# First pair of heads loaded on two queues and projected first, activation table behind the loads

## Chip, cores and metric

One core of a Trainium2 chip runs the kernel. The metric is the device time of one execution in microseconds (us), the median of several.

## What is computed

Linear attention over 8 batches and 8 heads of 576 tokens (64 wide) and then a mixture of experts on the 4608 rows that come out. Cut to what matters here:

```python
def phi(x):                                   # x: q or k, (8, 8, 576, 64)
    proj = einsum('bhsd,df->bhsf', x, w_phi)  # w_phi: 64 x 128
    proj = proj - max(abs(proj), axis=-1)
    return concat([exp(proj), exp(-proj)])
q_p, k_p = phi(q), phi(k)
kv  = einsum('bhsf,bhsd->bhfd', k_p, v)
z   = sum(k_p, axis=2)
num = einsum('bhsf,bhfd->bhsd', q_p, kv)
den = einsum('bhsf,bhf->bhs', q_p, z) + 1e-6
x   = num / den, as rows of 512               # 4608 x 512
# then: rows with x @ w_skip > 0 go through the expert of the largest gate
# logit (512 -> 1024 -> 512, relu), all others pass unchanged
```

## The kernel before

The attention goes through 16 units of four heads (`units["k"]`, `units["q"]`); a unit is two pairs of heads, numbered pr 0 and 1. The last tokens of each head (2 of every 18) are kept apart: they make a third, small piece of each unit, the tails, whose tiles end in t (`xTt`, `ut`, `ekt`).

- **Loads.** `st_load` (L330) brings a unit of k or q into `raw`. The first units come in eight DMAs of 72 KB, four for each pair (two heads by two halves of 32 columns), at L347; from unit 2 on k comes in four DMAs of 280 KB (L343). `st_loadv` brings v in five DMAs (L355 four times, L361). All are issued by SyncE (its queue is SPq), but for the first units: the second pair of the first k unit (argument `more`) and the whole first q unit are issued by ScalarE (ACTq), which also loads `w_phi` into `wsrc` (L824) ahead of them.
- **DMA semaphores.** The DMAs of both queues use eight semaphores in turn, DMAHW0 to DMAHW7, in the order in which the scheduler places them. A DMA that gets a semaphore a second time is issued only when the DMA that had it before has landed.
- **Projection.** VectorE transposes `raw` into `xT` (pair) and `xTt` (tails of the unit) at L384. `st_proj` multiplies them by `wsrc` on TensorE (L395) into one of two PSUM buffers `ps_A`, and VectorE takes the largest magnitude (`m`, L405) and subtracts it (`u`, L406), which frees `ps_A`. The third projection in a row therefore waits until `u` (or `ut`) of the first is done.
- **Use.** ScalarE makes `ekt` and `ek` from `ut` and `u` (L420). TensorE sums them with v into `ps_K` (`st_use_k`, L476). For q, `u` is transposed and used against the sums (L428, L545).
- **Order.** The main loop runs steps t = 0, 1, 2, ...; each step handles one pair of k and one of q (two steps later), and the letters of `CFG["order"]`, alternating by the parity of t, say in what order its pieces are emitted: `0` is the projection of the tails, `1` that of a k pair, `2` that of a q pair, `a`, `b`, `c`, `d` VectorE's work for them. `CFG["ends"]` replaces the string for single steps. Steps 0 to 2 are still ordered by the scheduler; from step 3 on the order written here stands.
- **Activation table.** A one-element `Exp` on the tile `warm` (L105), ahead of everything on ScalarE, brings the table in early.

The functions that the change touches:

Of the kernel before, what the change touches and what calls it, by code (L numbers as in the profile page):

```python
# [13 lines left out]
AF = mybir.ActivationFunctionType  # L14
# [4 lines left out]

P = 128  # L20
SLOT = 256
CFG = {'late': 1, 'sp': 1, 'gp': (6, 8, 11, 14, 16, 19, 21), 'rows': 9.0, 'tab': (2, 2, 3, 4, 5, 6, 7, 8, 9, 10, 11, 12, 15, 19, 31), 'ql': 0, 'cp': 0, 'seq': ('E', 'E', 'E', 'C', 'C', 'SC', 'C', 'DS', 'C', 'D'), 'post': (4, 8, 6), 'post2': (3, 5, 5), 'pk': (0, 2, 4), 'man': (3, 38), 'eng': ('PE', 'DVE', 'Activation', 'Pool'), 'nb': {'K': 1, 'O': 1, 'A': 2, 'P': 3, 'U': 2}, 'apools': (('ld', 2), ('hl', 4), ('up', 5), ('zp', 2), ('ep', 7), ('kvp', 5), ('ac', 1), ('xp', 3)), 'mpools': (('wseta', 1), ('mx', 1), ('mo', 2), ('wsetb', 1), ('wsetc', 1), ('rawq', 1)), 'lag': (2, 2, 3, 0), 'order': ('LPv12KQebRcdBuExzwlr', 'LP01aKQ2ebRcdBuExwzyr'), 'vl': 0, 'at': 1, 'eb': (2, 2), 'ub': 4, 'stage': (2, 2, 4, 4), 'stage2': (1, 2, 3, 3), 'dve': ('0', '1', 'ntkq', '2', 'n2', 'tkq', 'n2t'), 'pd': 1, 'vq': 0, 'qq': 1, 'xb': 4, 'whole': 'k', 'vb': 1, 'af': 1, 'wg': 2, 'q0': 1, 'out6': 2, 'ends': {34: '2dcvQeuEFBwlLRPr', 35: 'QcueERwyLXPr', 36: 'cuwRyLPr'}}


@with_exitstack
def kernel(
# [256 lines left out]
    with actx:  # L285
        ld, hl, zp, up, ep, kvp, xp = (pools[nm] for nm in ("ld", "hl", "zp", "up", "ep", "kvp", "xp"))
# [17 lines left out]
        units = {"k": [], "q": []}  # L304
        for b in range(B):
            for hq in range(NQ):
                for kind in ("k", "q"):
                    u = Unit()
# [18 lines left out]
                c.pop(0)()  # L327
                last = c

        def st_load(u, eng=nc.sync, more=None):  # L330
            whole = u.kind in CFG["whole"]
            w = D if whole else 32
            whole = whole and u.g >= CFG["wg"]
            u.raw = ld.tile([P, 2, 18, w], F32, tag="raw" + u.kind, name="raw", bufs=2)
            for pr in range(1 if whole else 2):
                for hd in range(2):
                    for dh in range(2):
                        r = slice((2 * hd + dh) * 32, (2 * hd + dh) * 32 + 32)
                        src = kv_in[u.kind][u.g][hd * 32:hd * 32 + 32]
                        if whole:  # L340

                            n = 18 * D - 32
                            nc.sync.dma_start(  # L343
                                out=u.raw[r].rearrange("p r t c -> p r (t c)")[:, :, 0:n],
                                in_=src[:, :, dh * 32:dh * 32 + n])
                        else:
                            (more if more and pr == 1 else eng).dma_start(  # L347
                                out=u.raw[r, pr, :, 0:32],
                                in_=src[:, pr].rearrange("p (t c) -> p t c", c=D)[:, :, dh * 32:dh * 32 + 32])

# [483 lines left out]
        man = None
        pend = []
        for t in range(NPR + F + LQ + 2):
            if t == CFG["man"][0]:
                man = ExitStack()
# [33 lines left out]
            qx, mx, kb = [], {}, []  # L872
# [386 lines left out]
    for grp in CFG["seq"]:  # L1259
# [17 lines left out]
    order = sorted(begin, key=begin.get)  # L1277
# [48 lines left out]
    two = [x for x in order if x[0] != "S"]  # L1326
# [125 lines left out]
```

## Time and profile before

| | us |
|---|---|
| median of 3 runs | 581.87 (579.68 to 582.03) |
| the profiled execution, its own time | 578.38 |
| its span, first to last instruction | 576.2 |
| TensorE busy | 522.2 (91%) |
| VectorE busy | 447.4 (78%) |
| ScalarE busy | 341.9 (59%) |
| GpSimd busy | 282.7 (49%) |

The span leaves out 2.2 us around the first and last instruction. Busy shares are means over the whole kernel, the attention and the experts together; the change lies within its first steps, so the rows that matter are those of the first 40 us.

### The profile page before, as it was taken

What the parts mean: (1) busy time and instruction counts of PE and PEld (TensorE: products, weight loads), DVE (VectorE), ACT (ScalarE), POOL (GpSimd) and SP (SyncE); (2) the same over time, 40 slices, a digit from 0 to 9 for tenths busy, and PEclk for the clock granted to TensorE, in tenths of its full rate; (3) what the DMA queues carried; (4) which work ended last, traced back from release to release, by engine and by line L of the source; (5) the groups of instructions that cost most, each with busy time, mean ns of one, the idle gap of its engine ahead of it and who ended that gap; (6) DMA issues with size and microseconds to landing.
All of it is one profiled execution on the core that took longest, in us unless ns stands there. A gap on an engine that the chain in (4) does not pass through costs nothing. (4 is left out here: it accounts for less than half of the span.)

```text
span 576.2 us, 20682 instructions
## 1 busy us (share of the span) xinstructions
PE 522.2 (91%) x8606; PEld 485.4 (84%) x8606; DVE 447.4 (78%) x790; ACT 341.9 (59%) x606; POOL 282.7 (49%) x520
## 2 busy tenths in 40 slices
PE   2888999998999898998989999799999989999993
PEld 2788999888998888998988898699889878988892
DVE  3887788988778887797966897778879898868840
ACT  1457676677666776677665443745676757646620
POOL 4213335635547354564546256683749571558011
PEclk9989999999999999999999999899999999999998
DMA  7878878788987989875367895679577986867400
GB/s 147 176 166 163 168 160 211 194 170 174 243 205 194 195 174 224 201 183 122 130 211 270 251 335 179 180 247 335 167 254 241 325 289 233 276 205 250 171 20 32
DMA packets 151233, 116.25 MB, mean 202 GB/s; under 512 B 91875, under 2 KB 126819, under 8 KB 150114
## 3 DMA queue, kind: packets, MB, share of 16 engines
q1 hardware_dynamic: 140704, 104.51, 66.7%
q0 software_dynamic: 3200, 9.45, 4.6%
q10 hardware_dynamic: 7234, 0.95, 1.0%
q8 instruction: 69, 1.13, 0.8%
q14 instruction: 26, 0.21, 0.1%
HBM read 91.66 MB, written 24.02 MB: 201 GB/s over the span
## 5 line engine op out<-in xcount | busy, mean ns | idle before, releaser
L217 POOL TENSOR_TENSOR w<-wraw_c,w 128x256 fp32r<-128x256 f32 x84 | 81.1, 994 | 54.2 <-ACT w L212 38.4
L405 DVE TENSOR_REDUCE m<-ps_A 128x8 f32<-128x1024 f32 x64 | 77.0, 1203 | 35.7 <-PE ps_A L395 35.7
L217 DVE TENSOR_TENSOR w<-wraw_c,w 128x1024 fp32r<-128x1024 f32 x71 | 94.0, 1340 | 12.8 <-ACT w L212 12.5
L212 ACT ACTIVATE w<-wraw_c 128x1024 fp32r<-128x1024 f32 x92 | 93.8, 1050 | 7.4 <-DMA wraw_c<-in_moe_w_dram 7.4
L476 PE MATMUL ps_K<-vm,ek 128*64 128x65 f32 x2048 | 79.9, 224 | 5.4 <-issue 3.0
L406 DVE TENSOR_TENSOR u<-ps_A,m 128x1024 f32<-128x1024 f32 x64 | 78.3, 1224 | 3.9
L545 PE MATMUL ps_O<-kva,eq 128*64 128x74 f32 x1984 | 76.8, 229 | 4.6 <-issue 4.0
L395 PE MATMUL ps_A<-wsrc,xT 64*128 64x128 f32 x1024 | 73.1, 289 | 7.2 <-DVE u L406 4.5
L476 PEld LDWEIGHTS ps_K<-vm,ek 128*64 128x64 f32 x2048 | 73.0, 140 | 5.5 <-issue 4.7
L545 PEld LDWEIGHTS ps_O<-kva,eq 128*64 128x64 f32 x1984 | 68.8, 136 | 8.2 <-issue 4.6
L395 PEld LDWEIGHTS ps_A<-wsrc,xT 64*128 64x128 f32 x1024 | 65.8, 199 | 10.2 <-DVE u L406 4.8
L437 ACT ACTIVATE eq<-ps_V 128x1024 f32<-128x1024 f32 x64 | 65.7, 1030 | 9.6 <-PE ps_V L428 9.6
L420 ACT ACTIVATE ek<-u 128x1024 f32<-128x1024 f32 x64 | 64.1, 1057 | 2.3 <-DVE u L406 2.3
L1110 PE MATMUL ps_O<-w,hh 128*128 128x512 f32 x160 | 63.7, 398 | 0.0
L1029 POOL DMA_INDIRECT out_dram<-o,si x22 | 28.8, 1307 | 59.5 <-DVE si L1025 46.0
L549 ACT ACTIVATE os<-ps_O 128x296 f32<-128x296 f32 x62 | 26.1, 420 | 48.4 <-PE ps_O L545 46.4
L1115 PE MATMUL ps_O<-w,hlo 128*128 128x512 f32 x120 | 47.2, 394 | 0.0
L1114 PE MATMUL ps_O<-w,hh 128*128 128x512 f32 x120 | 47.0, 391 | 0.0
L524 POOL TENSOR_TENSOR xm<-os,rec 128x512 f32<-128x512 f32 x32 | 33.4, 1045 | 24.9 <-DVE rec L523 21.5
L384 DVE STREAM_TRANSPOSE xT<-raw 128x512 f32<-128x512 f32 x64 | 40.5, 669 | 1.2 <-DMA raw<-in_k_dram 1.2
L476 PE MATMUL ps_K<-vt,ekt 128*64 128x65 f32 x512 | 37.7, 224 | 0.0
L1110 PEld LDWEIGHTS ps_O<-w,hh 128*128 128x128 f32 x160 | 30.1, 188 | 6.1
(283 smaller groups left out, 1084.9 us busy)
## 6 DMA issues: line engine op xcount, KB each, us to landing
wraw_c<-in_moe_w_dram SPq DMA_DIRECT2D x96, 512.0 KB, 5.3
raw<-in_k_dram SPq DMA_DIRECT2D x56, 280.0 KB, 5.3
raw<-in_q_dram SPq DMA_DIRECT2D x120, 72.0 KB, 4.6
xrows<-xm SPq DMA_DIRECT2D x8, 1028.0 KB, 5.8
v<-in_v_dram SPq DMA_DIRECT2D x64, 128.0 KB, 3.4
out_dram<-xm SPq DMA_DIRECT2D x32, 256.0 KB, 4.8
xrows<-xt SPq DMA_DIRECT2D x4, 257.0 KB, 6.0
v<-in_v_dram SPq DMA_DIRECT2D x16, 64.0 KB, 3.1
```

The source lines that it names most:

```text
L212: nc.scalar.activation(out=hi, in_=raw, func=AF.Copy)
L217: eng.tensor_tensor(out=lo[:, r], in0=raw[:, r], in1=hi[:, r].bitcast(F32), op=ALU.subtract)
L395: nc.tensor.matmul(p[:, hd, j * NF:(j + 1) * NF], xT[r], wsrc[r], start=True, stop=True)
L405: lambda: nc.vector.tensor_reduce(out=m, in_=pv, axis=AX.X, op=ALU.max, apply_absolute_value=True),
L406: lambda: nc.vector.tensor_tensor(out=uu, in0=pv, in1=m.rearrange("p h (j o) -> p h j o", o=1).broadcast_to([P, 2, n, NF]), op=ALU.subtract),
L420: nc.scalar.activation(out=o, in_=uu, func=AF.Exp, scale=(1.0, -1.0)[a])
L437: return [lambda a=a: nc.scalar.activation(out=e[:, a].rearrange("p s g c -> p s (g c)"), in_=t, func=AF.Exp, scale=(1.0, -1.0)[a]) for a ...
L476: nc.tensor.matmul(o[s * 64:s * 64 + 64, hd, half, :], e[:, half, s * 64:s * 64 + 64], x, start=(g == 0), stop=(g == 4))
L545: q_last[0] = nc.tensor.matmul(ov[s * 64:s * 64 + 64, 2 * j + hd, :], e[:, half, s, 4 * hd + 2 * th + j], kva[:, half, 2 * pr + hd, :], st ...
L1110: nc.tensor.matmul(y[sub], hh[:, t], wh[:, fi, :], start=first, stop=False)
L1114: nc.tensor.matmul(y[sub], hh[:, t], wl[:, fi, :], start=False, stop=False)
L1115: nc.tensor.matmul(y[sub], hlo[:, t], wh[:, fi, :], start=False, stop=last)
```

## The change

It does four things. The first k unit's eight loads are dealt to the two queues by `CFG["k0"]`: of pair 0 three go to SyncE and one to ScalarE, of pair 1 two and two (before: four and four, by pair). The one-element `Exp` moves behind these loads in the program. In step t = 1 the pair's projection and its VectorE work (`1`, `b`) come ahead of the tails' (`0`, `a`). In the same string `z` and `w` change places, but neither emits anything in step 1.

`CFG` is one line in the source; of it only the end, where it differs, is shown.

```diff
-..., 'q0': 1, 'out6': 2, 'ends': {34: '2dcvQeuEFBwlLRPr', ...}}
+..., 'q0': 1, 'out6': 2, 'w0': 0, 'k0': ('0001', '0011'),
+ 'ends': {1: 'LP1b0aKQ2eRcdBuExzwyr', 34: '2dcvQeuEFBwlLRPr', ...}}
 # step 1 before, from 'order': 'LP01aKQ2ebRcdBuExwzyr'
...
     nc.vector.memset(warm, 0.0)
-    nc.scalar.activation(out=warm, in_=warm, func=AF.Exp)
+    if CFG["w0"]:
+        nc.scalar.activation(out=warm, in_=warm, func=AF.Exp)
...
-        def st_load(u, eng=nc.sync, more=None):
+        def st_load(u, eng=nc.sync, two=None):
...
-                            (more if more and pr == 1 else eng).dma_start(
+                            (two[pr][2 * hd + dh] if two else eng).dma_start(
...
-        st_load(units["k"][0], more=nc.scalar)
+
+        st_load(units["k"][0], two=[[(nc.sync, nc.scalar)[int(c)] for c in o] for o in CFG["k0"]])
+        if not CFG["w0"]:
+            nc.scalar.activation(out=warm, in_=warm, func=AF.Exp)
```

**TensorE, its first instructions** (`ps_A` is a projection's result, `xT` a pair, `xTt` the tails). Before:

```order
L395 MATMUL ps_A<-wsrc,xTt 128x128 [waits DMAHW0_49,DVE_49]
L395 MATMUL ps_A<-wsrc,xTt 128x128
L395 MATMUL ps_A<-wsrc,xT 128x128 x8
L395 MATMUL ps_A<-wsrc,xT 128x128 [waits DVE_49,PE_49]
L395 MATMUL ps_A<-wsrc,xT 128x128 x7
L476 MATMUL ps_K<-vm_109,ek 64x65 [waits Activation_49,Pool_49]
```

Now:

```order
L395 MATMUL ps_A<-wsrc,xT 128x128 [waits DMAHW0_49,DVE_49]
L395 MATMUL ps_A<-wsrc,xT 128x128 x7
L395 MATMUL ps_A<-wsrc,xTt 128x128 [waits DVE_49]
L395 MATMUL ps_A<-wsrc,xTt 128x128
L395 MATMUL ps_A<-wsrc,xT 128x128 [waits DVE_49,PE_49]
L395 MATMUL ps_A<-wsrc,xT 128x128 x7
```

Pair 0 has moved ahead of the tails. The third projection, that of pair 1, reuses the buffer of the first: before that was the tails', now it is pair 0's.

**VectorE, from its first transposition on** (`m` and `u` belong to a pair, `mt` and `ut` to the tails). Before:

```order
L384 STREAM_TRANSPOSE xT<-raw 128x4x4x32 [waits DMAHW4_49,DMAHW6_49,DMAHW2_49,DMAHW1_49]
L384 STREAM_TRANSPOSE xTt<-raw 128x128 [waits DMAHW5_49,DMAHW7_49,DMAHW3_49,DMAHW1_49]
L384 STREAM_TRANSPOSE xT<-raw 128x4x4x32
L405 TENSOR_REDUCE mt<-ps_A 128x2 [waits PE_49]
L406 TENSOR_TENSOR ut<-ps_A,mt 128x2x128 [waits DVE_49]
L405 TENSOR_REDUCE m<-ps_A 128x8 [waits PE_49]
L406 TENSOR_TENSOR u<-ps_A,m 128x1024 [waits DVE_49]
L405 TENSOR_REDUCE m<-ps_A 128x8 [waits PE_49]
L384 STREAM_TRANSPOSE xT<-raw 128x4x4x32 [waits DMAHW4_49,DMAHW6_49,DMAHW2_49,DMAHW0_49]
L384 STREAM_TRANSPOSE xT<-raw 128x4x4x32 [waits DMAHW5_49,DMAHW7_49,DMAHW3_49,DMAHW1_49]
L406 TENSOR_TENSOR u<-ps_A,m 128x1024 [waits DVE_49]
```

Now:

```order
L384 STREAM_TRANSPOSE xT<-raw 128x4x4x32 [waits DMAHW3_49,DMAHW4_49,DMAHW2_49,DMAHW1_49]
L384 STREAM_TRANSPOSE xTt<-raw 128x128 [waits DMAHW6_49,DMAHW7_49,DMAHW5_49,DMAHW0_49]
L384 STREAM_TRANSPOSE xT<-raw 128x4x4x32
L405 TENSOR_REDUCE m<-ps_A 128x8 [waits PE_49]
L405 TENSOR_REDUCE mt<-ps_A 128x2 [waits PE_49]
L406 TENSOR_TENSOR u<-ps_A,m 128x1024 [waits DVE_49]
L406 TENSOR_TENSOR ut<-ps_A,mt 128x2x128 [waits DVE_49]
L405 TENSOR_REDUCE m<-ps_A 128x8 [waits PE_49]
L384 STREAM_TRANSPOSE xT<-raw 128x4x4x32 [waits DMAHW4_49,DMAHW6_49,DMAHW1_49,DMAHW0_49]
L406 TENSOR_TENSOR u<-ps_A,m 128x1024 [waits DVE_49]
L384 STREAM_TRANSPOSE xT<-raw 128x4x4x32 [waits DMAHW7_49,DMAHW5_49,DMAHW3_49]
```

The three transpositions of the first unit keep their places; `m` of pair 0 now stands right behind them, and one of the two later transpositions has moved behind the second `u`.

**SyncE's queue from its first load** (`raw` is k, `v` is v; the eight loads behind the first unit's v are the second k unit). Before:

```order
L347 DMA raw<-in_k_dram 32x18x32 x4
L355 DMA v<-in_v_dram 32x4x256 [waits DMAHW0_49]
L355 DMA v<-in_v_dram 32x4x256 [waits DMAHW2_49]
L355 DMA v<-in_v_dram 32x4x256 [waits DMAHW4_49]
L355 DMA v<-in_v_dram 32x4x256 [waits DMAHW6_49]
L361 DMA v_170<-in_v_dram 32x4x128 [waits DMAHW0_49]
L347 DMA raw<-in_k_dram 32x18x32 [waits DMAHW2_49]
L347 DMA raw<-in_k_dram 32x18x32 [waits DMAHW4_49]
L347 DMA raw<-in_k_dram 32x18x32 [waits DMAHW6_49]
L347 DMA raw<-in_k_dram 32x18x32 [waits DMAHW0_49]
```

Now:

```order
L347 DMA raw<-in_k_dram 32x18x32 x4
L347 DMA raw<-in_k_dram 32x18x32 [waits DMAHW0_49]
L355 DMA v<-in_v_dram 32x4x256 [waits DMAHW2_49]
L355 DMA v<-in_v_dram 32x4x256 [waits DMAHW4_49]
L355 DMA v<-in_v_dram 32x4x256 [waits DMAHW6_49]
L355 DMA v<-in_v_dram 32x4x256 [waits DMAHW0_49]
L361 DMA v_170<-in_v_dram 32x4x128 [waits DMAHW2_49]
L347 DMA raw<-in_k_dram 32x18x32 [waits DMAHW4_49]
L347 DMA raw<-in_k_dram 32x18x32 [waits DMAHW6_49]
L347 DMA raw<-in_k_dram 32x18x32 [waits DMAHW0_49]
L347 DMA raw<-in_k_dram 32x18x32 [waits DMAHW1_49]
```

SyncE issues five of the first unit's loads instead of four. The fifth has DMAHW0, which `wsrc` had first; everything behind it moves back by one place and by one semaphore. On ScalarE's queue the order is now `wsrc`, three k loads, the table and the `Exp`, eight q loads; before it was `wsrc`, the table and the `Exp`, four k loads, eight q loads, the fourth k load waiting for DMAHW1 (SyncE's first load). On no engine does any later instruction change its place.

## Rows read from the trace of the kernel before

**Rows 1.** From the waits of the first 30 us: engine, line and tile that waited, what for, us in total, times, longest.

```profile
PE ps_A L395 <- DVE xTt L384: 9.3, 1, 9.3
```

**Rows 2.** The timeline of the first 24 us, the rows of SyncE's and ScalarE's queues and of the table load: start, us, engine, line, what, count.

```profile
0.80 1.18 ACTq L824 DMA_DIRECT2D wsrc<-in_w_phi_dram  x1
0.81 2.97 SPq L347 DMA_DIRECT2D raw<-in_k_dram  x4
...
2.01 1.28 ACT L105 ACT_TABLE_LOAD   x1 [2.01 <-issue]
2.08 1.33 ACTq L347 DMA_DIRECT2D raw<-in_k_dram  x2
...
3.30 0.20 ACT L105 ACTIVATE warm<-warm 128x1 f32<-128x1 f32 x1
3.44 2.52 ACTq L347 DMA_DIRECT2D raw<-in_k_dram  x2
...
5.18 2.35 SPq L355 DMA_DIRECT2D v<-in_v_dram  x4
...
6.00 6.75 ACTq L347 DMA_DIRECT2D raw<-in_q_dram  x8
```

**Rows 3.** The wait of SyncE's queue for `wsrc`, from the waits of that queue in the first 60 us, and single issues from timelines of single stretches: the last k load of ScalarE, and SyncE's third to fifth load of the second k unit.

```profile
SPq L355 <- DMA wsrc<-in_w_phi_dram: 1.4, 1, 1.4
...
5.37 0.59 ACTq L347 DMA_DIRECT2D raw<-in_k_dram  x1
...
10.71 2.33 SPq L347 DMA_DIRECT2D raw<-in_k_dram  x3
```

**Rows 4.** The same timeline of the first 24 us, rows of the engines; in brackets the idle time before a row and what ended it.

```profile
7.32 0.71 DVE L384 STREAM_TRANSPOSE xT<-raw 128x512 f32<-128x512 f32 x1 [1.17 <-DMA raw<-in_k_dram]
...
8.89 0.31 DVE L384 STREAM_TRANSPOSE xTt<-raw 128x128 f32<-128x128 f32 x1 [0.86 <-DMA raw<-in_k_dram]
9.13 0.67 DVE L384 STREAM_TRANSPOSE xT<-raw 128x512 f32<-128x512 f32 x1
...
9.85 3.62 PE L395 MATMUL ps_A<-wsrc,xT 64*128 64x128 f32 x32
10.10 0.42 DVE L405 TENSOR_REDUCE mt<-ps_A 128x2 f32<-128x256 f32 x1 [0.31 <-PE ps_A L395]
10.56 0.42 DVE L406 TENSOR_TENSOR ut<-ps_A,mt 128x256 f32<-128x256 f32 x1
10.79 1.04 POOL L366 COPY vm<-v 128x1024 f32<-128x1024 f32 x1 [4.68 <-DMA v<-in_v_dram]
...
11.81 1.23 DVE L405 TENSOR_REDUCE m<-ps_A 128x8 f32<-128x1024 f32 x1 [0.82 <-PE ps_A L395]
12.80 0.72 ACT L420 ACTIVATE ekt<-ut 128x256 f32<-128x256 f32 x2 [9.29 <-DMA raw<-in_q_dram]
13.07 1.23 DVE L406 TENSOR_TENSOR u<-ps_A,m 128x1024 f32<-128x1024 f32 x1
14.21 1.21 DVE L405 TENSOR_REDUCE m<-ps_A 128x8 f32<-128x1024 f32 x1
14.33 2.00 ACT L420 ACTIVATE ek<-u 128x1024 f32<-128x1024 f32 x2 [0.81 <-DVE u L406]
15.34 1.29 DVE L384 STREAM_TRANSPOSE xT<-raw 128x512 f32<-128x512 f32 x2
...
15.53 1.14 PE L476 MATMUL ps_K<-vm,ek 128*64 128x65 f32 x16 [2.06 <-ACT ek L420]
...
17.67 0.48 DVE L384 STREAM_TRANSPOSE xTt<-raw 128x128 f32<-128x128 f32 x2
...
19.42 0.72 PE L395 MATMUL ps_A<-wsrc,xTt 64*128 64x128 f32 x8
...
20.18 0.69 DVE L405 TENSOR_REDUCE mt<-ps_A 128x4 f32<-128x512 f32 x1 [2.03 <-PE ps_A L395]
```

**Rows 5.** SyncE's queue from the timeline of 15 to 30 us: the four loads of the third k unit (280 KB each) and the eight of the second q unit.

```profile
19.66 1.79 SPq L343 DMA_DIRECT2D raw<-in_k_dram  x4
21.49 7.85 SPq L347 DMA_DIRECT2D raw<-in_q_dram  x8
```

**Rows 6.** VectorE from the timeline of 26 to 40 us.

```profile
31.51 0.31 DVE L384 STREAM_TRANSPOSE xTt<-raw 128x128 f32<-128x128 f32 x1 [0.94 <-DMA raw<-in_q_dram]
...
34.22 1.22 DVE L406 TENSOR_TENSOR u<-ps_A,m 128x1024 f32<-128x1024 f32 x1
```

**Rows 7.** TensorE from the timeline of 28 to 40 us.

```profile
27.71 1.16 PE L395 MATMUL ps_A<-wsrc,xT 64*128 64x128 f32 x16
...
35.59 2.03 PE L395 MATMUL ps_A<-wsrc,xT 64*128 64x128 f32 x16 [1.30 <-DVE u L406]
```

**Rows 8.** Busy time by stretches: from:to, its length, then busy us (and instructions) of TensorE, its weight loads, VectorE, ScalarE and GpSimd, the granted TensorE clock, the DMA share, GB/s.

```profile
18.60:25.40 6.80, 6.08 (x151) 5.66 (x150) 5.15 (x7) 1.46 (x3) 2.62 (x7) 1.00 0.89 214
...
35.60:39.20 3.60, 3.60 (x42) 3.60 (x44) 2.57 (x4) 0.90 (x2) 2.14 (x5) 0.53 1.07 215
```

**Rows 9.** DMA issues of 6 to 12.7 us: what, queue, count, KB each, median us from issue to landing.

```profile
raw<-in_q_dram ACTq DMA_DIRECT2D x8, 72.0 KB, 3.4
v<-in_v_dram SPq DMA_DIRECT2D x3, 128.0 KB, 3.4
```

More of the change, by code (lines that the diff above doesn't have):

```diff
@@ L21 @@
 SLOT = 256
-CFG = {'late': 1, 'sp': 1, 'gp': (6, 8, 11, 14, 16, 19, 21), 'rows': 9.0, 'tab': (2, 2, 3, 4, 5, 6, 7, 8, 9, 10, 11, 12, 15, 19, 31), 'ql': 0, 'cp': 0, 'seq': ('E', 'E', 'E', 'C', 'C', 'SC', 'C', 'DS', 'C', 'D'), 'post': (4, 8, 6), 'post2': (3, 5, 5), 'pk': (0, 2, 4), 'man': (3, 38), 'eng': ('PE', 'DVE', 'Activation', 'Pool'), 'nb': {'K': 1, 'O': 1, 'A': 2, 'P': 3, 'U': 2}, 'apools': (('ld', 2), ('hl', 4), ('up', 5), ('zp', 2), ('ep', 7), ('kvp', 5), ('ac', 1), ('xp', 3)), 'mpools': (('wseta', 1), ('mx', 1), ('mo', 2), ('wsetb', 1), ('wsetc', 1), ('rawq', 1)), 'lag': (2, 2, 3, 0), 'order': ('LPv12KQebRcdBuExzwlr', 'LP01aKQ2ebRcdBuExwzyr'), 'vl': 0, 'at': 1, 'eb': (2, 2), 'ub': 4, 'stage': (2, 2, 4, 4), 'stage2': (1, 2, 3, 3), 'dve': ('0', '1', 'ntkq', '2', 'n2', 'tkq', 'n2t'), 'pd': 1, 'vq': 0, 'qq': 1, 'xb': 4, 'whole': 'k', 'vb': 1, 'af': 1, 'wg': 2, 'q0': 1, 'out6': 2, 'ends': {34: '2dcvQeuEFBwlLRPr', 35: 'QcueERwyLXPr', 36: 'cuwRyLPr'}}
+CFG = {'late': 1, 'sp': 1, 'gp': (6, 8, 11, 14, 16, 19, 21), 'rows': 9.0, 'tab': (2, 2, 3, 4, 5, 6, 7, 8, 9, 10, 11, 12, 15, 19, 31), 'ql': 0, 'cp': 0, 'seq': ('E', 'E', 'E', 'C', 'C', 'SC', 'C', 'DS', 'C', 'D'), 'post': (4, 8, 6), 'post2': (3, 5, 5), 'pk': (0, 2, 4), 'man': (3, 38), 'eng': ('PE', 'DVE', 'Activation', 'Pool'), 'nb': {'K': 1, 'O': 1, 'A': 2, 'P': 3, 'U': 2}, 'apools': (('ld', 2), ('hl', 4), ('up', 5), ('zp', 2), ('ep', 7), ('kvp', 5), ('ac', 1), ('xp', 3)), 'mpools': (('wseta', 1), ('mx', 1), ('mo', 2), ('wsetb', 1), ('wsetc', 1), ('rawq', 1)), 'lag': (2, 2, 3, 0), 'order': ('LPv12KQebRcdBuExzwlr', 'LP01aKQ2ebRcdBuExwzyr'), 'vl': 0, 'at': 1, 'eb': (2, 2), 'ub': 4, 'stage': (2, 2, 4, 4), 'stage2': (1, 2, 3, 3), 'dve': ('0', '1', 'ntkq', '2', 'n2', 'tkq', 'n2t'), 'pd': 1, 'vq': 0, 'qq': 1, 'xb': 4, 'whole': 'k', 'vb': 1, 'af': 1, 'wg': 2, 'q0': 1, 'out6': 2, 'w0': 0, 'k0': ('0001', '0011'), 'ends': {1: 'LP1b0aKQ2eRcdBuExzwyr', 34: '2dcvQeuEFBwlLRPr', 35: 'QcueERwyLXPr', 36: 'cuwRyLPr'}}
 @with_exitstack
```

## Prediction

> **What bounds the kernel now.** The busy shares of the whole span name no stage, so I read the first 40 us only, in this order: what TensorE waits for first, the queues, the engines, and then the first place where a load is late again. TensorE's longest wait is its first, 9.3 us for the tails' transposition [rows 1]. The reader is to see that this wait ends with the last of eight loads: VectorE transposes pair 0 at 7.32, then stands still for 0.86 us until all eight have landed, and starts `xTt` at 8.89 [rows 4]. The last load is late because it is issued late: ScalarE's third and fourth k load take 2.52 us together, and the fourth goes out only at 5.37 [rows 2, 3], though the third began at 3.44. It waits for SyncE's first load to land, because the semaphores go round.
>
> From 9.85 on TensorE, VectorE and ScalarE take turns, to 20.18, where VectorE has waited 2.03 us for the next tails [rows 4]. The place that decides my sum comes later: at 31.51 VectorE has waited 0.94 us for the second q unit's loads [rows 6]. What it does then ends with a `u` at 34.22 + 1.22 = 35.44, for which TensorE has idled 1.30 us until 35.59 [rows 6, 7]. So in this execution the start as a whole is worth what it does to that load: the engines had 0.94 us to spare there, the queue had none.
>
> **The first loads.** SyncE's four loads take 2.97 us, 0.74 each [rows 2]. Pair 0 now needs three of them and one of ScalarE's, so its transposition can start one issue earlier, 7.32 − 0.74 = 6.6, and ends at 7.3. The eighth load is now SyncE's fifth. It has the semaphore of `wsrc`, and the row of the v load, which waited for that until 5.18 [rows 2, 3], says when it goes: 5.18 instead of 5.37. So `xTt` starts at 8.7 instead of 8.89, and the second `xT` ends at 9.6 instead of 9.80.
>
> **The table load.** It takes 1.28 us and the `Exp` 0.20, to 3.50; yet ScalarE's first k loads go out from 2.08, while it runs, and the third at 3.44 [rows 2]. So it held nothing up, and taking it out of the way of the loads gains nothing. Behind the loads it could hold the q loads at worst until 3.44 + 0.65 + 1.48 = 5.6 (0.65 is half of the 1.33 for two loads), still earlier than their 6.00 [rows 2]; I take 5.4, when SyncE's first load has landed. The Trainium skill (ScalarE: Activation LUTs, What ACT_TABLE_LOAD costs) states about 2.66 us for a load with its drain; by that the q loads would begin at an estimated 6.8, later than before. The row of 1.28 and the loads issued beside it speak against it; it is a rival below.
>
> **The projections.** Pair 0's matmuls take half of the 3.62 us of thirty-two, 1.8 [rows 4], at the lower of the two clock levels (later sixteen take 1.16 [rows 7]): 7.3 to 9.1, all of it ahead of VectorE, which first has the other two transpositions until 9.6. Then `m` 1.23, `mt` 0.42, `u` 1.23, `ut` 0.42 [rows 4]: `u` is ready at 12.5 instead of 14.30, `ut` at 12.9 instead of 10.98. But pair 1's matmuls now want pair 0's buffer and wait for that `u`: 12.5 to 14.3, where before they ran on without a gap. So the second `m` starts at 14.3, not earlier than its 14.21 [rows 4]: of 1.8 us nothing is left on VectorE. Behind it now come `xT`, `u`, `xT` and `xTt` twice, 3.7 us after 15.5 as before, or later if the second k unit is late (below): 18.5 to 18.9 instead of 18.15.
>
> **The first sums.** ScalarE's `ekt` waits for `ut`: 12.9 to 13.6; the first `ek` ends a microsecond later, at 14.65, and TensorE's `ps_K` starts there instead of at 15.53, 0.88 earlier. GpSimd's copy of v, done at 11.83 [rows 4], covers this unless the fourth v load (next paragraph) pushes it past 14.6; it is what is late next. The sums take 3.9 us (15.53 to 19.42), so the tails follow at 18.55, or at 18.9 when `xTt` is later. Against 19.42 that is a gain of **0.5 to 0.87 us for the engines**; I take 0.5, by the later transposition.
>
> **SyncE's queue.** Here the change costs. The fifth k load is one issue, 0.74, in front of everything else. More: the fourth v load now waits for that k load to land, so it goes at 8.7 and not before 5.18 + 2.35 = 7.5, and the third load of the second k unit waits for that v load. With 3.4 us to landing [rows 9] that is 12.1 instead of 10.71 [rows 3], 1.4 late. From there to the second q unit, at 21.49, the queue hardly rests [rows 2, 5]. So the delay lies between 0.74 and 1.4. I take **0.9**, nearer to the single issue, because the loads that follow have waited a little as well (eight q loads took 6.75 us, 0.84 each [rows 2], against 0.74) and can close up. The second k unit is then late by about 0.9 too, and takes the 0.4 us from the engines that I have counted. The delay goes on: the 280 KB loads behind it start at 19.66 + 0.9, the second q unit at 21.49 + 0.9 [rows 5], and its last load lands at 31.5 + 0.9 = 32.4.
>
> The Trainium skill (DMA: Bandwidth & Descriptors, Issuing engines are not separate DMA queues) says that loads issued on several engines run on the same sixteen DMA engines, and that only issue time is saved. By it pair 0 would still be transposed at 7.32 and the second sum start some 0.2 us later than above; the end would not move, since the q loads set it.
>
> **Sum.** VectorE comes to its wait 0.5 us earlier and is let go 0.9 us later. Everything behind it, to TensorE at 35.59 and on, moves with it: **+0.9 us**, bounds −0.87 (the queue is not late and the engines decide) and +1.4. No later instruction changes place. The profiled execution took 578.38 us by itself, 3.5 below the median of the runs, 581.87; the four executions lie between 578.38 and 582.03. I put the sum on their middle, (579.68 + 581.87)/2 = 580.8, which gives **581.7**.
>
> **The rivals.**
> *The engines decide at 31.5.* For it: only 0.94 us separate the two chains [rows 6], and an execution in which the higher clock comes later than here leaves the queue more room. Against it: the row as it stands. Then the gain is what the engines keep, 0.5: 580.3.
>
> *The clock is kinder.* From 35.6 to 39.2 the granted clock averages 0.53, and TensorE is busy throughout [rows 8]; at the higher level sixteen matmuls take 1.16 for 2.03 [rows 7], so these 3.6 us would be 2.1. If that stretch is not granted low, 1.5 go, with the engines' 0.5: 580.8 − 2.0 = 578.8. For it: the idle 1.30 us just before it would lie elsewhere. Against it: by my sum the idle gets longer.
>
> *The clock is worse, and the kernel slower.* The wait for `u` leaves TensorE idle from about 9.7 to 12.5, where before it worked until 13.47. Should the higher level therefore come only at 25.4, the 6.08 us of work from 18.6 on [rows 8] take 6.08 × 2.03/1.16 = 10.6, 4.6 more, less 0.72 of idle there and the 0.94: +2.9. With the low stretch at 35.6 doubled, +1.5 more: 585.2. It decides only if both happen; TensorE's sums, gapless from 14.65, speak against it.
>
> *The table holds the q loads.* Should it take twice its 1.28 there and hold the queue meanwhile, the q loads begin at 4.1 + 2.56 + 0.20 = 6.9; the fifth, which waits for the first, goes at 10.3 and lands at 13.7 [rows 9]. SyncE's fourth load of the second k unit waits for that and would otherwise go at about 12.9, so 0.8 is added to the 0.9: 580.8 + 1.7 = 582.5. Against it: the loads issued beside the table load [rows 2]. The Trainium skill's figure, named above, would do nearly the same.
>
> **How the numbers follow.** Forecast 0.52, engines decide 0.25, kinder clock 0.12, worse clock 0.06, table 0.05. Half a per cent, about what a measurement of this kernel can tell from no change, is 2.9 us: below 579.0 or above 584.8. Only the kinder clock reaches the first, and the spread of runs around the others adds what it misses: faster 0.12. Only the worse clock reaches the second: slower 0.05. Same: 0.83. The range goes from the kinder clock with the engines' full gain, 580.8 − 0.87 − 1.5 = 578.4, to the slowest run with the queue's upper bound, 582.03 + 1.4 = 583.4.
>
> **What would show it.** Right: TensorE starts near 7.3 and idles before pair 1 until `u` is done at 12.5; `ps_K` starts near 14.7; SyncE begins the 280 KB loads near 20.5; VectorE waits over 1.5 us for the second q unit and goes on near 32.4. Wrong: the fourth v load going out near 7.2, the 280 KB loads at 19.7 or earlier, or a VectorE that no longer waits for that unit. A change of over 3 us without a difference in the low-clock stretches would overthrow the whole sum.

## The result, and the profile after

The change made the kernel slower. It took 584.03 us (median of 22 runs, 580.41 to 588.12), the kernel before beside it 581.27 (22 runs, 577.97 to 583.61): ratio 1.0053 with a 95% interval of 1.0035 to 1.007, some 3 us. The prediction was 581.7, inside half a per cent, with a range to 583.4. The profiled execution took 585.84 by itself (span 583.6), that of before 578.38, so the two lie on opposite sides of their medians, and late differences between them are not all the change's.

The first 24 us of the changed kernel answer to [rows 2] and [rows 4]: start, us, engine, line, what, in brackets the idle time before and what ended it.

```profile
0.80 4.81 SPq L347 DMA_DIRECT2D raw<-in_k_dram  x5
...
2.01 2.07 ACTq L347 DMA_DIRECT2D raw<-in_k_dram  x3
...
4.11 1.28 ACT L828 ACT_TABLE_LOAD   x1 [4.11 <-issue]
...
5.27 0.57 ACTq L347 DMA_DIRECT2D raw<-in_q_dram  x1
...
6.48 0.71 DVE L384 STREAM_TRANSPOSE xT<-raw 128x512 f32<-128x512 f32 x1 [0.33 <-DMA raw<-in_k_dram]
...
7.25 2.08 PE L395 MATMUL ps_A<-wsrc,xT 64*128 64x128 f32 x16 [7.25 <-DMA raw<-in_k_dram]
7.47 0.31 DVE L384 STREAM_TRANSPOSE xTt<-raw 128x128 f32<-128x128 f32 x1 [0.28 <-DMA raw<-in_k_dram]
...
12.21 2.08 PE L395 MATMUL ps_A<-wsrc,xT 64*128 64x128 f32 x16 [2.45 <-DVE u L406]
...
14.39 1.13 PE L476 MATMUL ps_K<-vm,ek 128*64 128x65 f32 x16
...
18.46 0.71 PE L395 MATMUL ps_A<-wsrc,xTt 64*128 64x128 f32 x8 [1.05 <-DVE xTt L384]
...
19.21 0.69 DVE L405 TENSOR_REDUCE mt<-ps_A 128x4 f32<-128x512 f32 x1 [0.71 <-PE ps_A L395]
```

TensorE starts at 7.25 for 9.85, waits for `u` before pair 1, and `mt` comes at 19.21 for 20.18: the engines are 0.97 us earlier. The start does what it was made to do. SyncE's queue, from the timeline of 15 to 30 us, answers to [rows 5]:

```profile
20.47 1.78 SPq L343 DMA_DIRECT2D raw<-in_k_dram  x4
22.30 8.30 SPq L347 DMA_DIRECT2D raw<-in_q_dram  x8
```

It is 0.81 us later. Where the two meet, VectorE in the timeline of 26 to 46 us answers to [rows 6]:

```profile
29.29 0.30 DVE L384 STREAM_TRANSPOSE xTt<-raw 128x128 f32<-128x128 f32 x1
33.95 0.31 DVE L384 STREAM_TRANSPOSE xTt<-raw 128x128 f32<-128x128 f32 x1 [4.35 <-DMA raw<-in_q_dram]
...
36.66 1.22 DVE L406 TENSOR_TENSOR u<-ps_A,m 128x1024 f32<-128x1024 f32 x1
```

The wait has grown from 0.94 to 4.35 us. VectorE comes 0.97 earlier and goes on 2.44 later, at 33.95 for 31.51. TensorE, from the timeline of 28 to 46 us, answers to [rows 7]:

```profile
34.32 0.49 PE L395 MATMUL ps_A<-wsrc,xTt 64*128 64x128 f32 x4 [1.22 <-DVE xTt L384]
...
38.03 2.08 PE L395 MATMUL ps_A<-wsrc,xT 64*128 64x128 f32 x16 [3.22 <-DVE u L406]
...
40.72 2.05 PE L395 MATMUL ps_A<-wsrc,xT 64*128 64x128 f32 x16
...
42.70 1.25 PE L545 MATMUL ps_O<-kva,eq 128*64 128x74 f32 x32
```

It idles 3.22 us for 1.30, and what follows runs at the lower clock for twice as long. The windows of the changed kernel answer to [rows 8] (TensorE's granted clock is the figure behind the five engines):

```profile
35.60:39.20 3.60, 1.17 (x10) 1.20 (x12) 3.46 (x4) 0.00 (x0) 2.13 (x5) 0.54 1.00 246
35.90:42.70 6.80, 4.67 (x48) 4.48 (x48) 5.62 (x7) 1.02 (x1) 2.13 (x5) 0.50 1.04 207
```

0.50 of full speed, the 1.2 GHz level, holds from 35.9 to 42.7; before it held from 35.7 to 39.1. The first `L545` stands at 42.70; in the kernel before it stands here, in the same view:

```profile
39.70 1.25 PE L545 MATMUL ps_O<-kva,eq 128*64 128x74 f32 x32
```

So 3.0 us are lost by there, which is the size of the median loss. In these two executions not all of it lasts: a later `u` of VectorE is 1.71 us behind before's, and at the end of the span the two are 7.4 apart. From the timelines of 62 to 81 us, before and then the change:

```profile
77.96 1.22 DVE L406 TENSOR_TENSOR u<-ps_A,m 128x1024 f32<-128x1024 f32 x1
```

```profile
79.67 1.23 DVE L406 TENSOR_TENSOR u<-ps_A,m 128x1024 f32<-128x1024 f32 x1
```

What made the load 2.44 late rather than 0.9 shows in its landing events: fifteen of its sixteen parts are in by 32.42, 0.94 later than before's last; the sixteenth comes at 33.92. What else the DMA engines did then, from the DMA view of 31.8 to 32.9 us (packets, MB, share):

```profile
q1 hardware_dynamic: 407, 0.22, 84.9%
q8 instruction: 1, 0.02, 5.3%
```

One packet of 16 KB, an instruction fetch, begins at 31.88 and takes 0.93. Before, its counterpart began at 32.84, after the load had landed at 31.48. That the fetch is TensorE's is inferred below; the view names the queue (q8) and no engine.

### The profile page after: what moved, and what is told of

Same layout as the page of the kernel before. It is cut to its first block, busy times and chain, and to the rows that moved or that the text cites. A ratio compares the mean times of both kernels' runs of the same rounds, so it can differ in the third digit from the quotient of the medians.

```text
span 583.6 us, 20680 instructions
## 1 busy us (share of the span) xinstructions
PE 526.3 (90%) x8606; PEld 485.9 (83%) x8606; DVE 445.2 (76%) x790; ACT 341.5 (59%) x606; POOL 281.3 (48%) x520
## 5 line engine op out<-in xcount | busy, mean ns | idle before, releaser
L217 DVE TENSOR_TENSOR w<-wraw_c,w 128x1024 fp32r<-128x1024 f32 x71 | 95.6, 1363 | 14.8 <-ACT w L212 13.8
L545 PE MATMUL ps_O<-kva,eq 128*64 128x74 f32 x1984 | 76.9, 229 | 4.3 <-issue 3.7
L545 PEld LDWEIGHTS ps_O<-kva,eq 128*64 128x64 f32 x1984 | 68.9, 136 | 8.0 <-issue 4.2
```

What stands on the lines that cost most here:

```text
L217: eng.tensor_tensor(out=lo[:, r], in0=raw[:, r], in1=hi[:, r].bitcast(F32), op=ALU.subtract)
L545: q_last[0] = nc.tensor.matmul(ov[s * 64:s * 64 + 64, 2 * j + hd, :], e[:, half, s, 4 * hd + 2 * th + j], kva[:, half, 2 * pr + hd, :], st ...
```

## Experiments

Theory 1: SyncE's queue, one load longer, makes the second q unit late, its last part comes later still (1a), and the idle that grows in front of it brings the longer low clock. Its rival: the new order, the moved table or the engines' shift costs, and the loads nothing. Later runs part theory 1 further, under letters that their expectations explain.

Edits are against the changed kernel, or against the kernel before where that is said. Ratios are to the kernel before on the same chip. The table has what the stage around the second q unit showed in each profile: when VectorE went on (`xTt`), its wait, TensorE's idle time before the pair's `xT` matmuls, the low granted clock that came within or behind it, then the ratio. Times are us.

| kernel | xTt | wait | idle | low clock | ratio (95%) |
|---|---|---|---|---|---|
| before | 31.51 | 0.94 | 1.30 | 3.4 | 1 |
| the change | 33.95 | 4.35 | 3.22 | 6.8 | 1.0053 (1.0035 to 1.007) |
| e1_loads_undone | 30.41 | 1.07 | 1.43 | 3.4 | 1.0002 (0.9979 to 1.0025) |
| e2_loads_only | 34.32 | 4.34 | 3.22 | 6.8 | 1.0029 (1.0002 to 1.0057) |
| e3_four_four | 31.09 | 1.51 | 1.87 | 3.4 | 0.9993 (0.997 to 1.0016) |
| e17, the same again | 30.85 | 1.41 | 1.77 | none | 1.0011 (0.9986 to 1.0036) |
| e4_gate_pool | 32.43 | 1.61 | 1.97 | 6.8 | 1.0032 (1.0011 to 1.0054) |
| e8_four_four_gate | 31.73 | 1.72 | 2.08 | 3.4 | 0.9987 (0.9953 to 1.0021) |
| e6_six_two | 34.20 | 3.92 | 3.22 | 6.8 | 1.003 (0.9991 to 1.0069) |
| e5_look1, the change | 33.38 | 4.08 | 3.23 | 6.8 | one run |
| e11, the change | 33.92 | 4.16 | 3.23 | 3.4 | 1.0046 (1.0024 to 1.0068) |
| e9_fetch_after | 32.76 | 1.07 | 2.31 | 3.4 | 1.001 (0.9988 to 1.0032) |
| e14_fetch_after_22 | 32.71 | 2.98 | 3.22 | 6.8 | 1.0076 (1.0047 to 1.0105) |
| e10_fetch_before | 31.6 | 0 | 0.39 | 3.4, at 17.5 | 1.001 (0.9978 to 1.0042) |
| e12_fetch_before_22 | 32.15 | 1.66 | 2.02 | 6.8 | 1.0055 (1.003 to 1.008) |
| e13_fetch_before_30 | 32.07 | 2.14 | 2.50 | 6.8 | 1.0082 (1.005 to 1.0113) |
| e7_fill | 32.02 | 0.79 | 0 | none | 1.0072 (1.004 to 1.0104) |
| e15_fill_nine | 32.35 | 0.88 | 0 | none | 0.9995 (0.9975 to 1.0015) |
| e16_four_four_fill | 31.08 | 1.47 | 0.52 | none | 0.9995 (0.9974 to 1.0016) |

### Which part costs

**e1_loads_undone** deals the loads by pair again and keeps the new order and the moved table; **e2_loads_only** keeps the deal and undoes the other two; **e3_four_four** (and e17) gives ScalarE one load more, so that SyncE issues four.

```diff
-'w0': 0, 'k0': ('0001', '0011'), 'ends': {1: 'LP1b0aKQ2eRcdBuExwzyr', ...
+'w0': 0, 'k0': ('0000', '1111'), 'ends': {1: 'LP1b0aKQ2eRcdBuExwzyr', ...   # e1
+'w0': 1, 'k0': ('0001', '0011'), 'ends': {...                               # e2
+'w0': 0, 'k0': ('0001', '0111'), 'ends': {1: 'LP1b0aKQ2eRcdBuExwzyr', ...   # e3, e17
```

Expected, in this order:

> The changed kernel with the first unit's loads dealt as before (four and four by pair); projection order and table load stay changed. Theory 1 (SyncE's queue, one load longer, brings the second q unit late): the 280 KB loads start near 19.7 as before, the second q unit has landed by 31.5, VectorE waits about 1.9 us for it instead of 4.35, and the time is that of before within 0.7 us. Theory 2 (the new order of the projections costs, by TensorE's idle time before pair 1): still about 2.8 us over before.

> The loads alone: dealt as in the change (five and three), with the projection order and the place of the table load of before. Theory 1: 280 KB loads near 20.5, the second q unit at 32.4 or later, about 2 to 3 us over before. Theory 2: the time of before.

> The change with one load given back: pair 0 still three and one, pair 1 one and three, so each queue issues four. Order and table as changed. Theory 1: SyncE's queue as before, the second q unit by 31.5, the time of before within 0.7 us, and pair 0 still transposed near 6.5. Theory 2: about 2.8 us over before.

> The four and four deal alone, beside the other two on their chip: 0.997 to 1.001 of before, VectorE's wait for the second q unit 1.2 to 1.9 us, one low stretch of 3.4 us near 35.

The 280 KB loads began at 18.54 in e1, 20.23 in e2 and 19.13 in e3, and the wait and the time go with them: with four loads on SyncE the kernel is as before, with five it is slower, whatever the order and the table. That the fifth load is needed for the loss is shown by e1 and e3; that it is enough rests on e2, whose interval begins at 1.0002. e17 missed one thing: no low stretch came near 35. The three kernels with four loads give the engines' gain (e1's `xTt` at 30.41 is 1.1 earlier than before's) and still no time below before that the intervals could tell.

### Other levers on the queue

**e4_gate_pool** moves the two `wgs` loads (L144, L145) from SyncE to GpSimd; **e8_four_four_gate** does so with the deal of e3; **e6_six_two** deals six loads to SyncE.

```diff
-nc.sync.dma_start(out=wgs[:, :, 0:E], ...)      # and the next line
+nc.gpsimd.dma_start(out=wgs[:, :, 0:E], ...)    # e4, e8
-'k0': ('0001', '0011')
+'k0': ('0001', '0111')                          # e8
+'k0': ('0001', '0001')                          # e6
```

> The whole change, but the two loads of the gate and skip weights (wgs) are issued by GpSimd instead of SyncE, so SyncE's queue is two issues (1.3 us) shorter ahead of the 280 KB loads. Theory 1: these start near 19.2, the second q unit has landed near 31.2, VectorE waits near 1.6 us, and the time is that of before within 0.7 us or under it. Theory 2: about 2.8 us over before.

> Four loads on each queue (pair 0 three and one, pair 1 one and three), and the two loads of wgs issued by GpSimd, the rest as changed. Theory 1: the 280 KB loads start near 17.9, the second q unit has landed near 29.8, VectorE waits under 0.8 us for it, and the time is 0.7 to 1.5 us under before. Rival (the engines decide by then, or GpSimd's copy of v comes late behind wgs): the time of before within 0.5 us.

> One more load on SyncE: six of the first unit's eight loads there, two on ScalarE; all else as changed. Theory 1 (SyncE's queue sets the second q unit): the 280 KB loads start 0.6 to 0.8 us later than with five (near 21.2), VectorE goes on that much later or more, and the time is 0.5 to 1.5 us above the change. Rival (the number of loads on the queue is not what counts, some other part of the new dealing is): the time of the change within 0.4 us.

e4 missed: the 280 KB loads came only 0.56 earlier than in the change (19.91), and the engines 1.2 later. `ps_K` began at 15.33 instead of 14.39, because ScalarE made `ekt` only behind its last q loads, at 13.52 instead of 12.57, and `ek` behind it; GpSimd's copy of v, at 12.81 behind that of `wgs` (L149, 12.20), was done by 13.85 and held nothing. e8 (18.30) is not told from before. e4 and e8 differ by one load as the change and e3 do, and they point the same way: neither has a late part, their waits are alike (1.61 and 1.72), and e4, with five loads, has the long low stretch and the higher ratio; but the two intervals overlap. e6 has its 280 KB loads at 21.19, as expected (the change's profiles have them at 19.89 to 20.69), but its interval reaches from below before's time to that of the change, so it says nothing of what the sixth load costs.

### The late sixteenth part

The change ran twice more, unaltered: **e5_look1** and, timed beside the next two, **e11_after_again**.

> The changed kernel once more, for another profile of it. Theory 1a (the second q unit's last load lands late not by the queue alone but because an instruction fetch of 16 KB runs on one of its DMA engines near 31.9 us, each time): VectorE waits until about 34 again. Theory 1b (that was a chance of one execution): it goes on near 32.4.

> The change word for word, timed beside the other two on their chip. All theories: 1.003 to 1.007 of before, the 280 KB loads at 19.9 to 20.5, the fetch at 31.3 to 32.1, VectorE's xTt at 33.4 to 34.3 after a wait of over 4 us, and 6.8 us of low granted clock from about 36.

The late part came back: fifteen parts at 31.84 and the last at 33.36 in e5, with the fetch at 31.31; 32.37 and 33.90 in e11, fetch at 31.85; 32.38 and 34.30 in e2, fetch at 32.12. In the trace the fetch begins when TensorE has started 386 instructions (matmuls themselves not counted), in eight of the first ten profiles, of before (32.84) and of the change (31.88) alike; the count is 370 and 374 in the other two, and 350 to 388 in the nine later ones, added instructions included. That it is TensorE's is inferred from this. It goes with the engines: what made TensorE earlier brought the fetch onto a load that had become later.

To move the fetch, one-element matmuls were put on TensorE ahead of everything, where it idles; the order of all else stays. **e9_fetch_after** and **e10_fetch_before** have 46 of them in the changed kernel and in that before, **e12** and **e13** 22 and 30 in that before, **e14** 22 in the change.

```diff
+cold = const.tile([P, 1], F32, name="cold"); nc.vector.memset(cold, 0.0); fill = bank("O")
+[nc.tensor.matmul(fill[0:1, 0:1], cold, cold, start=True, stop=True) for _ in range(46)]   # 22, 30
 nc.scalar.dma_start(out=wsrc, ...)
```

> The change, with 46 one-element matmuls on a zero tile put on TensorE ahead of its first projection, where it idles; they move nothing else, and leave every load as it is. In eight of ten profiles so far the 16 KB instruction fetch near 32 us begins when TensorE has started 386 instructions, so it goes with the engines, not with the queue. With 46 more it should begin when the program's own 340th has started, near 30 us instead of 31.88. Theory A (the fetch holds back one sixteenth of the second q unit's last load): all sixteen parts land together near 32.4, VectorE's xTt starts at 32.4 to 32.8 instead of 33.95, TensorE's xT at 36.5 to 37.1 instead of 38.03, and the time is 1 to 2 us below the change run beside it. Rival B (the last part is late by the load's own length, whatever is fetched): xTt stays at 33.4 to 34.3 and the time within 0.5 us of the change's. Rival C (the fetch holds its DMA engine's ring back for good): the part stays late although the fetch is early, as under B, but with the fetch moved.

> The kernel before, with the same 46 one-element matmuls ahead of TensorE's first projection, and its loads untouched. The fetch that began at 32.84, after the second q unit's last load had landed (31.48), should begin near 30.9. Theory A: it falls on that load; one of sixteen parts lands 1 to 1.5 us late, VectorE's xTt starts at 32.4 to 33.0 instead of 31.51, TensorE's xT at 36.5 to 37.2 instead of 35.59, with a low granted clock behind it that lasts longer than the 3.4 us, and the kernel is 1 to 2.5 us slower than before without any change in its loads. Rivals B and C: xTt at 31.3 to 31.7, time within 0.5 us of before.

> The kernel before with 22 one-element matmuls ahead of TensorE's first projection, its loads untouched. The run with 46 had shown that each is two instructions (92 in all), and its fetch, at 29.33, came ahead of the second q unit's last load and held one part of the load before it (others landed by 30.06, that part at 31.46). With 44 instructions the fetch should begin when the program's own 342nd starts, at 30.9 to 31.6. Theory A (the fetch alone costs): it falls on the last load, whose last part then lands at 32.4 to 33.0 instead of 31.48; VectorE's xTt at 32.4 to 33.1, TensorE's xT at 36.4 to 37.2, time 1.001 to 1.004 of before. Rival (only a queue that is late as well gives the straggler): xTt at 31.3 to 31.8, time within 0.1% or so of before.

> The same with 30 matmuls, 60 instructions: the fetch at the program's own 326th, 30.4 to 31.3, in case the engines run as late as in the run with 46. Theory A: if it begins between 30.6 and 31.3, as with 22; if earlier, it holds a part of the load before the last, and VectorE goes on at 31.3 to 31.8, time as before. Rival: no straggler on the last load in either.

> The change with 22 such matmuls: the fetch at the program's own 342nd, 30.0 to 30.7 instead of 31.9, so ahead of the second q unit's last load (others at 32.3 to 32.7). Theory A: as with 46, the sixteen parts land together, VectorE's xTt at 32.4 to 32.9 after a wait of 1 to 3 us, time 1.000 to 1.003 of before, against 1.0046 without the matmuls. Rival (with 46 the gain came from TensorE running later there, not from the fetch): TensorE runs as in the change, xTt at 33.4 to 34.3, time 1.003 to 1.007 of before.

First the load. e9 and e14 have the fetch at 29.66 and 28.57, ahead of it, and the sixteen parts landed together, by 32.74 and 32.68. From the timelines of 26 to 46 us, e9 and then e14:

```profile
31.38 0.30 DVE L384 STREAM_TRANSPOSE xTt<-raw 128x128 f32<-128x128 f32 x1
32.76 0.31 DVE L384 STREAM_TRANSPOSE xTt<-raw 128x128 f32<-128x128 f32 x1 [1.07 <-DMA raw<-in_q_dram]
...
36.84 2.08 PE L395 MATMUL ps_A<-wsrc,xT 64*128 64x128 f32 x16 [2.31 <-DVE u L406]
```

```profile
29.42 0.30 DVE L384 STREAM_TRANSPOSE xTt<-raw 128x128 f32<-128x128 f32 x1
32.71 0.31 DVE L384 STREAM_TRANSPOSE xTt<-raw 128x128 f32<-128x128 f32 x1 [2.98 <-DMA raw<-in_q_dram]
...
36.79 2.08 PE L395 MATMUL ps_A<-wsrc,xT 64*128 64x128 f32 x16 [3.22 <-DVE u L406]
```

Both go on 1.2 us earlier than the change. And e12, the kernel before with its loads untouched, has the fetch at 30.09 and one part at 32.12 where the others are in by 30.63:

```profile
30.18 0.30 DVE L384 STREAM_TRANSPOSE xTt<-raw 128x128 f32<-128x128 f32 x1
32.15 0.31 DVE L384 STREAM_TRANSPOSE xTt<-raw 128x128 f32<-128x128 f32 x1 [1.66 <-DMA raw<-in_q_dram]
...
36.23 2.08 PE L395 MATMUL ps_A<-wsrc,xT 64*128 64x128 f32 x16 [2.02 <-DVE u L406]
```

So theory A holds for the load: a fetch that falls on it makes one part 1.5 us late, and a fetch that is moved off takes that away. e7 and e15 below agree: five loads on SyncE, fetches at 32.58 and 32.86, behind the load, and all parts together. That it is one and the same DMA engine is inferred; the records don't name it. e10 missed its aim: each of these matmuls is two instructions, the fetch came at 29.33, and held one part of an earlier load (31.46 for 30.06) that nobody waited for. In e13 it came at 28.91 and held no part of the last two loads for over 0.3 us; yet `xTt` came at 32.07, where 31.3 to 31.8 was expected.

Then the time, and here the runs don't agree. e9 took 3.4 us less than the change beside it (578.1 for 581.52), more than theory A had promised; e14 (six executions, no change beside it) was no faster than the change is elsewhere, and e12 with 1.0055 was slower than the 1.001 to 1.004 expected. e9 and e14 let VectorE go on at the same moment, 32.76 and 32.71, and their ratios are 1.001 and 1.0076, with intervals that don't touch. In e9 TensorE stood still for 1.12 us at 27.04, and VectorE came to the wait 2.0 later than in e14; that engines which come early cost time would fit. But the number of added matmuls fits as well, and so does the chip: the three kernels with 22 or 30 ran on one chip and are all slow, the two with 46 on another and are as before, whichever kernel they were added to. No run parts these.

The profiles point elsewhere than to the early engines. e9 and e13 start the first `L545` at the same moment, with ratios of 1.001 and 1.0082. From their timelines of 38 to 46 us:

```profile
40.82 1.25 PE L545 MATMUL ps_O<-kva,eq 128*64 128x74 f32 x32
```

```profile
40.82 1.70 PE L545 MATMUL ps_O<-kva,eq 128*64 128x74 f32 x32
```

The two are level until a `u` at 53.6 us. Then TensorE stops in e13, inside a run of sixteen matmuls, and in e14 inside a run of eight (timelines of 52 to 60 us), and both fall some 2 us further behind before:

```profile
56.05 0.64 PE L500 MATMUL ps_K<-wgd,kvt 128*64 128x18 f32 x15 [1.87 <-issue]
```

```profile
56.74 0.60 PE L395 MATMUL ps_A<-wsrc,xTt 64*128 64x128 f32 x6 [1.78 <-issue]
```

"issue" says that TensorE waited for nothing that the profile shows. A 16 KB fetch had begun at 53.48 and 54.03, 2.6 and 2.7 us before TensorE went on. All nineteen profiles have such stops: 89 of over 0.5 us between 12 and 330 us, 2 to 9 in each, and every one ends 2.2 to 3.1 us after such a fetch began. So a fetch seems to hold TensorE itself too, and matmuls put ahead move the places where it does; the stop of e9 at 27.04 is one of them. That the fetch is the cause is inferred from the times.

What the late part alone is worth is therefore not shown, nor that engines made earlier cost anything. e14's windows show that after its gain of 1.2 the long low stretch is there all the same, and another comes at 58.2, 1.5 us behind the stop.

```profile
34.30:41.10 6.80, 4.31 (x47) 4.34 (x48) 5.62 (x6) 1.69 (x2) 2.14 (x5) 0.50 1.08 215
58.20:61.60 3.40, 3.40 (x43) 3.18 (x41) 3.28 (x5) 1.02 (x1) 0.00 (x0) 0.50 0.69 156
```

### The clock

**e7_fill** puts ten 128x128 matmuls of the identity, twice, into step 5, around the tails' projection; **e15_fill_nine** nine, only where TensorE idles for `u`; **e16_four_four_fill** five there, with the deal of e3. Their results are not used.

```diff
-'ends': {1: 'LP1b0aKQ2eRcdBuExwzyr', 34: ...
+'ends': {1: 'LP1b0aKQ2eRcdBuExwzyr', 5: 'LPD0D1aKQ2ebRcdBuExwzyr', 34: ...   # e7
+'ends': {1: 'LP1b0aKQ2eRcdBuExwzyr', 5: 'LP0D1aKQ2ebRcdBuExwzyr', 34: ...    # e15, e16
...
+elif c == "D":
+    fill = bank("O")
+    for _ in range(10):                                              # 9, 5
+        nc.tensor.matmul(fill[:, 0:P], ident, ident, start=True, stop=True)
```

> The change with twenty matmuls of the identity into an unused bank, ten before and ten behind the tails' projection of step 5, where TensorE idles 1.2 and 3.2 us; their results are not read. VectorE's wait stays at 4.35 us. If the low granted clock from 36 us on is owed to that idle time and costs part of the loss: the clock stays high there, and the time is 1 to 2 us below the change. If the clock has no part in the loss: the time of the change within 0.4 us, or a little above.

> The change with nine 128x128 matmuls of the identity in step 5, between the tails' projection and that of the pair, where TensorE idles 3.22 us; at 0.25 us each they take 2.2 and end before the u it waits for, and no load is moved. Theory C (the low granted clock behind that idle is a good part of the loss): no low clock from 36 to 43, the sixteen xT matmuls take 1.16 instead of 2.08, TensorE's use of the next sums 1.5 to 2.5 us earlier than in the change, time 1.000 to 1.003 of before. Rival D (the clock takes its low stretch later, or the idle alone is the loss): the low stretch appears within the next 30 us, or the time stays at 1.004 to 1.007.

> The change with the first unit's loads dealt four and four (pair 0: three on SyncE and one on ScalarE, pair 1: one and three), and five such matmuls at the same place, 1.25 us of the 1.9 that TensorE idles there. Theory C: the low stretch of 3.4 us at 35 goes, 1 to 1.7 us less than without them: 0.996 to 0.998 of before. Rival D: 0.998 to 1.002, with a low stretch a little later.

e7 settled nothing: its low clock went, but its two groups of 2.50 us ran past the wait, and TensorE came to `xT` at 39.74. e15 tells more. From its timeline of 26 to 46 us, and its windows:

```profile
35.12 2.27 PE L941 MATMUL ps_O<-ident 128*128 128x128 f32 x18
37.33 1.16 PE L395 MATMUL ps_A<-wsrc,xT 64*128 64x128 f32 x16
...
39.86 1.25 PE L545 MATMUL ps_O<-kva,eq 128*64 128x74 f32 x32
```

```profile
36.00:43.00 7.00, 7.00 (x161) 6.76 (x161) 5.94 (x8) 3.07 (x4) 1.90 (x5) 1.00 1.02 187
```

The clock stays at its higher level, the sixteen matmuls take 1.16 instead of 2.08, and the first `L545` stands at 39.86 instead of 42.70. The time is 0.9995 of before: the whole loss of the change is back, with five loads on SyncE still. That is what theory C forecast, and the times of twelve executions show that the nine matmuls take the loss away. That they do it through the clock of this stage fits and is not shown, for three reasons. In this one profile the start ran at the lower clock for longer, past 20 us where the change had the higher one from 15.4, so the engines came late (a wait of 0.88) and the fetch, at 32.86, missed the load; the profile doesn't show the late part and the fill together. Its lead is also gone by 80 us: TensorE stops for 1.83 us, 2.7 after a fetch began, and `u` comes where the change has it (79.67). From its timelines of 64 to 77 and 62 to 81 us:

```profile
72.31 0.53 PE L500 MATMUL ps_K<-wgd,kvt 128*64 128x18 f32 x11 [1.83 <-issue]
```

```profile
79.82 1.22 DVE L406 TENSOR_TENSOR u<-ps_A,m 128x1024 f32<-128x1024 f32 x1
```

And nine matmuls are eighteen instructions that move every later fetch. The mean granted clock of the executions is 0.9885, where the change has 0.9825 (22 executions), e11 0.9829, and before 0.9854 to 0.9861 in four of the five comparisons (0.9830 in the other); but e7 has 0.9883 and e16 0.9882, and the one is slow and the other no faster than before. e16, without a low stretch here, gained nothing over e3 or before, where theory C had promised 1 to 1.7 us; e17, the same deal without the matmuls on the same chip, had none here either.

## Why the prediction was wrong

The direction and the places were right, the size was not, and the sum's last line failed. Of the 2.3 us between 581.7 and 584.03, 0.5 are the starting point: 580.8 was taken for before, and 581.27 was measured.

- **The first loads, the table, the projections: right.** Pair 0 is projected from 7.25 (predicted 7.3), TensorE idles for `u` until 12.21 (12.5), `ps_K` starts at 14.39 (14.65). `xTt` starts at 7.47, not 8.7, because the fifth load, issued at 5.05, landed by 7.45, after 2.4 us and not 3.4. The engines' gain is 0.97, not 0.5. The Trainium skill (DMA: Bandwidth & Descriptors, Issuing engines are not separate DMA queues) has it that a second issuing engine saves issue time alone; the row agrees, `xT` at 6.48 for 7.32, 0.84 and so about one issue. What I drew from it, that pair 0 would stay at 7.32, was wrong.
- **The table held nothing.** A q load went out at 5.27 while the table load ran from 4.11 to 5.39. The Trainium skill (ScalarE: Activation LUTs, What ACT_TABLE_LOAD costs) states some 2.66 us for a load with its drain; the row has 1.28 for the load, no drain shows behind it, and the queue did not stand still for it.
- **SyncE's queue: right in size, partly by luck.** 0.81 late at the 280 KB loads and 0.94 at fifteen parts of the q load, for 0.9. The way there was another: the fourth v load went at 7.47, not 8.7, nearer to the 7.2 that was named as a sign of being wrong, and the third load of the second k unit at 11.72, 1.0 late and not 1.4.
- **The term that failed** is the sum's "VectorE comes to its wait 0.5 us earlier and is let go 0.9 us later. Everything behind it, to TensorE at 35.59 and on, moves with it: **+0.9 us**". It measured +2.44 at VectorE and +3.0 at the first `L545`, against a loss of some 3 us in the whole. Two things were missing. The load's last part was late by 1.5 us more, through a fetch that the engines' gain had moved onto it; the trace of before had it 1.36 us behind the load, and I had not looked at it. And TensorE's idle time grew from 1.30 to 3.22 us, with 6.8 us of lower clock instead of 3.4, which adds the rest by `L545`. The sum moved everything behind the wait by the same amount and so priced that stretch at nothing, though the rivals held its price, 1.5 us.
- **The rivals.** "The clock is worse" had the doubled stretch, at +1.5, but only together with a late rise at the start: "It decides only if both happen". The rise was not late (15.4), the stretch doubled all the same, and the slower side came out at a chance of 0.05. "The engines decide", "the clock is kinder" and "the table holds the q loads" are out by the rows above.
- **What would overthrow it** was named: over 3 us without a difference in the low-clock stretches. The difference is there.

How the 3 us divide in the whole kernel stays open. Taking away the late part gave all in e9 and nothing in e14, covering the idle gave all in e15, in kernels whose later fetches and later low stretches moved too. What goes with the time best is the lower clock of the whole span. Added up from its first rise on, it takes 18.6 to 24.9 us in the profiles of the change, e2, e4, e6, e12, e13 and e14, and 11.4 to 15.8 in all others; of these only e7, with 12.2, is slow. The change has 22.0 us in its first profile for 14.9 of before; at 2.08 for 1.16 the 7.1 more are an estimated 3.1 us of work, but only 3.4 of them lie in this stage, the others come later (near 370 and 480 us), and no run shows what ties those to the change. That the deal of five loads starts the loss, by the queue and the wait, is shown by e1, e3 and e17, and by e2 as far as its interval goes.

## What to carry to other kernels

Where engines are made earlier in front of a transfer that isn't, their idle time grows: price it by what the granted clock did behind such idle times before, and look at what else comes earlier with the engines, instruction fetches among it. A load that moves to another queue lengthens that queue to the next place where it was already late; find that place first, and ask whether the queue can spare the issue. An experiment that adds instructions to TensorE changes more than the place where they stand, since the fetches behind them move: compare TensorE's stops before its time is read as the answer.

## What the runs showed of the hardware

- An instruction fetch (TensorE's, as inferred above) is one packet of 16 KB that took 0.93 to 1.42 us near 30 us, and where it fell on a load one of the load's sixteen parts landed 1.4 to 1.9 us behind the rest (the change in three profiles, e2, e10, e12; 0.8 and 1.3 in e6, where it fell between two loads).
- TensorE stopped for 0.5 to 1.9 us, 2 to 9 times in each profile between 12 and 330 us, waiting for nothing that the profile shows, and all 89 stops ended 2.2 to 3.1 us after a 16 KB fetch began.
- The lower clock came in stretches of 3.4 or 6.8 us in this stage, the longer one behind idle times of 1.97 to 3.23 us, the shorter behind 1.30 to 3.23 us: the idle time alone doesn't say which.
- ScalarE's queue issued a load while its activation table was being loaded, in both kernels (2.08 within 2.01 to 3.29 before, 5.27 within 4.11 to 5.39 after).
